# Column sums of w_out: eight slabs added on GpSimd ahead of two products, with a new table of keys

## The chip, the core and the metric

The program runs on one core of one Trainium2 chip. The metric is the device time of that core in microseconds (us), from the program's start to its end. The engines named here are TensorE (PE, with PEld for its weight loads), VectorE (DVE), ScalarE (ACT), GpSimd (POOL) and SyncE (SP), which issues nearly all DMA transfers here.

## What is computed

The kernel takes eight sequences of 3136 tokens by 256 features through a frequency-domain mix and then takes all 25088 tokens through a feed-forward layer.

```python
X = np.fft.rfft(x, axis=1)                 # 8 x 3136 x 256
Yr = Xr @ w_r - Xi @ w_i + b_r
Yi = Xr @ w_i + Xi @ w_r + b_i
Yr, Yi = soft_threshold(Yr, 0.01), soft_threshold(Yi, 0.01)
x = np.fft.irfft(Yr + 1j * Yi, n=3136, axis=1).reshape(25088, 256)
h = x @ w_in                               # 256 -> 1024
u = h * softmax(h)
ln = (u - mean(u)) / np.sqrt(var(u) + 1e-6) * g_ln
out = ln @ w_out                           # 1024 -> 256
```

`soft_threshold` shortens the name of three lines of the reference: sign times max(|y| - 0.01, 0).

## The kernel before

**Batches and tiles.** One batch is one sequence. The transforms are products with constant matrices in steps: `fwd1` (98 points, tiles of PSUM named `pf`, matrix `fa_s`), `fwd2` (32 points, matrix `fb`), the mix with `w_hi` and `w_lo`, the threshold, `inv1` (matrix `gb`, and `gs_s` for the last unit) and `inv2` (matrix `iaf_s` or `ia_s`), which fills a ring of token columns, `ring_hi` and `ring_lo`. Batch 0's transforms use the PSUM name `pb`, later ones `pf`. Each of 196 heads then takes 128 tokens out of the ring: `moe_head` makes `h` in two halves of 512 columns (six products each, PSUM name `ph`), VectorE finds the peak (`nm`), ScalarE the exponential (`u`, `se`), VectorE the product with it (`u`, `su`). `moe_turn` splits `u` into two float16 parts (`lh` on ScalarE, `ll` on GpSimd) that DMA transposes into `th` and `tl`. `moe_tail` multiplies these with `wout` in 24 products (PSUM name `po`) and scales the result (`o`). Data of 32 bits are carried as two 16-bit parts throughout, so most products come in threes.

**The first 130 us.** Batch 0 runs alone there, and the weights are made ready beside it. `fwd1_plain` of batch 1 is cut in eight chunks of `x` (tile `xt`, four buffers, shared with batch 0's bins) with two float32 products `pf<-xt,fa_s` each; `note_peak` reads each chunk for its peak, `x_scale` turns the peaks into a scale (`top`, a transpose on TensorE, then `v`, a product with `ones` that spreads it over the partitions). `moe_w_in` loads w_in in four pieces and `finish_w_in` splits it (`win_hi`, `win_lo`, `win_low`) when its peak is known (`wpeak`, `wtop`, `win_un`, `win_sc`). `moe_w_out` loads w_out in four pieces of two slabs, unpacks each with six VectorE instructions (on `lh`, `junk` and `ll`) and a GpSimd product, and multiplies the rows by `g_ln` (`gt`) on ScalarE. The four pieces lie in buffers named `th`, `tl`, `th`, `tl`.

**`finish_w_out`.** ScalarE takes the peak of each piece (`ll,mx`), `power_of_two` makes a scale of the four peaks through two small TensorE products with `wpeak` and `wtop`, and TensorE sums all 1024 rows of w_out into the column sums (eight float32 products `pf<-th,ones` and `pf<-tl,ones`). A float32 product leaves two MATMUL records in the trace. ScalarE writes the scaled sums into `o`; then each piece is scaled on ScalarE, GpSimd subtracts `o` from it, ScalarE casts the result to `wout[..., 0, :]` and GpSimd subtracts this for `wout[..., 1, :]`. No `po` product can start before the parts of `wout` that it reads are written.

**What sets the order.** Every operation carries a key (`nc.key`, from the table `KEYS`). A planner walks the operations by its own estimates of their lengths, takes for each engine the startable one with the smallest key within a patience of 50 ns, and writes each engine's program in the order found. Each engine then runs its own program strictly in that order and waits on semaphores where an input is not there. Buffers rotate by name: `u` has four, which w_in, the pieces of raw w_out and the heads share; `lh` and `ll` two each; `ph` may hold five of the eight PSUM banks, `po` two.

Of the kernel before, what the change touches and what calls it, by code (L numbers as in the profile page):

```python
# [12 lines left out]
F32 = mybir.dt.float32  # L13
# [28 lines left out]
def fft_constants():  # L42
# [73 lines left out]


KEYS = dict(
    slack_w=11.86, slack_1=3.28, slack_2=-1.08, gain=-179.81, xsc=-159.5, ssc=-155.78,
    b0=-187.72, b0_step=5.79, b0_mix=5.43, b0_inv=-16.84, b0_last=-31.78, in0=-155.58,  # L120
    in1=-179.39, in_end=-57.71, out=-132.55, out_step=3.47, out_peak=-55, out_sum=-54.6,
    out_end=-61.34, mixw=-54.7, a1=-96.85, a1_step=-0.23, a2=-73.62, a2_gap=-14.18, a=8.09,
    a_gap=10.32, b1=-74.41, b1_gap=4.59, b=-3.9, b_gap=1.01, f_mix=0, f_inv=0, back=-1.42,
    turn=1.77, tail=3.62,
)
K = KEYS.__getitem__

# [359 lines left out]
def fft_mix_solu_kernel(ctx: ExitStack, tc, x, w_r, w_i, b_r, b_i, w_in, w_out, g_ln, fa, iaf, fa16, fb, fs, gb, gs, ia, out):  # L487
    nc = Plan(tc.nc)
    B, _, D = x.shape
    FF = w_in.shape[1]  # L490
    P = 128
    ND = D // P
    NF = FF // P
# [10 lines left out]
    mp = Pool(ctx.enter_context(tc.tile_pool(name="mp", bufs=2)), 2)  # L504
# [3 lines left out]
    def front_psum(b):  # L508

        return banks.tile("pf" if b else "pb")  # L510
# [16 lines left out]
    ones = const.tile([P, P], F32, name="ones")  # L527
# [615 lines left out]
    pw = banks.tile("po")  # L1143
# [21 lines left out]
    pw = front_psum(0)  # L1165
# [3 lines left out]
    gain = const.tile([P, 1], F32, name="gain")  # L1169
# [33 lines left out]
    pw = front_psum(0)  # L1203
    nc.tensor.matmul(pw, ones[:1], bias_row.rearrange("p r e -> p (r e)"), start=True, stop=True)
    nc.scalar.copy(bias_t[:, :2].rearrange("p r e -> p (r e)"), pw)
    pw = front_psum(0)
# [43 lines left out]
    def power_of_two(peaks, un, sc, k):  # L1250

        top = sp.tile([P, 1], F32, name="wpeak", bufs=2)
        nc.vector.tensor_reduce(top, peaks, AX.X, ALU.max)
        pw = banks.tile("pf")
        nc.tensor.transpose(pw[:1, :P], top, ident)
        top = sp.tile([1, 1], F32, name="wtop", bufs=2)
        nc.vector.tensor_reduce(top, pw[:1, :P], AX.X, ALU.max)
        nc.vector.tensor_scalar(top, top, 2.0**-100, None, ALU.max)
        nc.vector.tensor_scalar(top.bitcast(U32), top.bitcast(U32), 0x7F800000, None, ALU.bitwise_and)
        pw = banks.tile("pf")  # L1260
        nc.tensor.matmul(pw[:, :1], ones[:1], top, start=True, stop=True)
        nc.vector.tensor_scalar(un, pw[:, :1], k, None, ALU.mult)
        nc.vector.tensor_scalar(sc.bitcast(U32), un.bitcast(U32), -1.0, float(254 << 23), ALU.mult, ALU.add)

    def moe_w_out():

        wo_s = [mp.tile([P, 2, D], F32, name=("th", "tl")[j % 2], bufs=3) for j in range(NF // 2)]
        rows = mp.tile([P, D], F32, name="o", bufs=2)[:NF, :P]
        nc.hold(raw[0, 3])
        nc.sync.dma_start(rows, g_ln.rearrange("(f p) -> f p", p=P))  # L1270
        pw = banks.tile("pf")
        nc.tensor.transpose(pw[:, :NF], rows, ident[:NF, :NF])
        gt = const.tile([P, NF], F32, name="gt")
        nc.vector.tensor_copy(gt, pw[:, :NF])
        for f in range(0, NF, 2):
            nc.key = K("out") + f * K("out_step")
            load_wide(wo_s[f // 2], w_out[f * P : (f + 2) * P].rearrange("(f p) e -> p f e", p=P), raw[0, 3])
            for i in (f, f + 1):
                row = wo_s[i // 2][:, i % 2]
                nc.scalar.activation(row, row, AF.Copy, scale=gt[:, i : i + 1])  # L1280
        return wo_s

    def finish_w_out(wo_s):

        nc.key = K("out_peak")
        mx = sp.tile([P, NF // 2], F32, name="mx", bufs=1)
        for j, half in enumerate(wo_s):
            junk = mp.tile([P, HF], BF16, name="ll", bufs=2)
            nc.scalar.activation(junk, half.rearrange("p f e -> p (f e)"), AF.Abs, accum_out=mx[:, j : j + 1])
        scale = sp.tile([P, 2], F32, name="scale", bufs=1)  # L1290
        power_of_two(mx, unscale, scale[:, :1], 2.0**-13)
        nc.vector.tensor_scalar(scale[:, 1:], scale[:, :1], 1.0 / FF, None, ALU.mult)
        nc.vector.tensor_scalar(unscale, unscale, 1e3 * W_SCALE, None, ALU.mult)
        nc.key = K("out_sum")
        pw = banks.tile("pf")
        with nc.together():
            for j in range(NF):
                nc.tensor.matmul(pw[:, :D], ones, wo_s[j // 2][:, j % 2], start=j == 0, stop=j == NF - 1)
        cm = mp.tile([P, D], F32, name="o", bufs=2)
        nc.scalar.activation(cm, pw[:, :D], AF.Copy, scale=scale[:, 1:])  # L1300

        nc.key = K("out_end")
        for j, half in enumerate(wo_s):
            fs = slice(2 * j, 2 * j + 2)
            nc.scalar.activation(half, half, AF.Copy, scale=scale[:, :1])
            for i in range(2):
                nc.gpsimd.tensor_sub(half[:, i], half[:, i], cm)
            nc.scalar.copy(wout[:, fs, 0], half)
            nc.gpsimd.tensor_sub(wout[:, fs, 1], half, wout[:, fs, 0])
# [42 lines left out]
    nc.key = K("out")  # L1352
    wo_s = moe_w_out()
    finish_w_out(wo_s)
    nc.key = K("mixw")
    later_mix_weights()
# [48 lines left out]
```

## Time and profile before

| | us |
|---|---|
| median of three runs (1524.37 to 1527.14) | 1526.11 |
| the profiled execution, whole | 1526.09 |
| its span, first to last instruction | 1524.3 |
| PE busy in the span | 1500.1 |
| DVE / ACT / POOL busy in the span | 1279.9 / 1245.1 / 1143.7 |

The profile is of one execution. A timeline row gives start, duration, engine, operation with what it writes and reads, and in brackets how long the engine sat idle before it and what ended that. A PE row's duration includes its drain, so the time that a product occupies the engine is read from the distance between starts. A row of the windows gives one stretch with each engine's busy time, the granted TensorE clock as a share of the higher of its two levels (2.4 and 1.2 GHz), and the DMA engines' mean busy share.

### The profile page before, as it was taken

To read this page: it belongs to the slowest core of one execution; us is meant where nothing else is said; L and a number is where in the kernel's file an instruction comes from. 1 tells how busy PE (TensorE), PEld (TensorE's weight loads), DVE (VectorE), ACT (ScalarE), POOL (GpSimd) and SP (SyncE) were. 2 spreads that over 40 slices of the span, in tenths; PEclk is the share of its full clock that TensorE was granted. 3 is DMA by queue.
4 is the path that set the end of the run, shared out by engine and by line. 5 is a ranking of instruction groups with operands and counts; after the bars stand their busy time and mean duration, and the time that the engine had idled before them with its cause. 6 is when DMAs were issued, how large, how long until landed. Compare 5 with 4: busy or idle time off the path is not lost.

```text
span 1524.3 us, 42130 instructions
## 1 busy us (share of the span) xinstructions
PE 1500.1 (98%) x15375; PEld 1060.9 (70%) x15375; DVE 1279.9 (84%) x3068; ACT 1245.1 (82%) x2548; POOL 1143.7 (75%) x1848
## 2 busy tenths in 40 slices
PE   6989999999999999999999999999999999999998
PEld 3446777667766777677766777667776777766676
DVE  5888899889998898978898888988989788776674
ACT  5789887998789878987888777887879788788886
POOL 0658998677977888569966788667986698867776
PEclk8989999999999999999999999999999999999999
DMA  8776977999679986999689996899769976687776
GB/s 265 226 225 154 172 168 175 240 233 222 162 169 229 233 192 141 260 216 215 143 171 234 233 189 142 185 246 225 158 140 213 224 143 114 140 174 140 143 129 115
DMA packets 531588, 285.69 MB, mean 187 GB/s; under 512 B 426500, under 2 KB 504688, under 8 KB 531380
## 3 DMA queue, kind: packets, MB, share of 16 engines
q1 hardware_dynamic: 530932, 281.39, 83.8%
q8 instruction: 120, 1.97, 0.6%
q10 hardware_dynamic: 448, 1.61, 0.4%
q14 instruction: 88, 0.72, 0.2%
HBM read 103.07 MB, written 77.07 MB: 118 GB/s over the span
## 4 chain that ended last, share of the span: by engine, by line
PE 90%; DVE 3%; ACT 2%; POOL 2%; DMA 2%; issue 1%; SPq 0%; DVEq 0%; ACTq 0%; POOLq 0%
PE po L375 31%; PE ph L375 31%; PE pf L375 24%; PE pb L375 3%; DMA u<-in_x_dram 1%; DVE xl L375 1%; POOL ll L375 1%; DVE nm L375 0%; DMA u<-in_moe_w_out_dram 0%; DVE u L375 0%; POOL wout L375 0%; DVE av L375 0%; DMA xt<-in_x_dram 0%; ACT w_hi L375 0%; POOL a L375 0%
## 5 line engine op out<-in xcount | busy, mean ns | idle before, releaser
L375 POOL TENSOR_TENSOR ll<-u,lh 128x1024 f16<-128x1024 f32 x196 | 424.9, 2168 | 88.8 <-ACT lh L375 86.8
L375 PE MATMUL po<-wout,th 128*128 128x256 f16 x3136 | 374.5, 273 | 0.0
L375 ACT ACTIVATE u<-ph,m,hsb 128x512 f32<-128x512 f32 x384 | 297.2, 782 | 77.2 <-DVE m L375 77.0
L375 DVE TENSOR_REDUCE nm<-ph 128x1 f32<-128x512 f32 x392 | 266.8, 687 | 104.9 <-PE ph L375 103.8
L375 PEld LDWEIGHTS <-th 128*128 128x128 f16 x3136 | 303.6, 98 | 56.6 <-issue 0.8
L375 DVE SCALAR_TENSOR_TENSOR u<-ph,ch,u 128x512 f32<-128x512 f32 x392 | 284.6, 748 | 38.5 <-ACT u L375 29.0
L375 PE MATMUL ph<-win_hi,ring_hi 128*128 128x512 f16 x768 | 291.2, 379 | 0.7 <-DVE u L375 0.5
L375 PE MATMUL ph<-win_low,ring_lo 128*128 128x512 f16 x768 | 291.0, 379 | 0.0
L375 PE MATMUL ph<-win_lo,ring_hi 128*128 128x512 f16 x768 | 291.0, 379 | 0.0
L375 ACT CAST lh<-u 128x1024 f16<-128x1024 f32 x196 | 206.6, 1055 | 50.9 <-DVE u L375 49.7
L375 PEld LDWEIGHTS <-ring_hi 128*128 128x128 f16 x1536 | 148.5, 98 | 137.4 <-issue 1.8
L375 ACT ACTIVATE junk<-u,total 128x1024 bf16<-128x1024 f32 x196 | 227.6, 1161 | 10.9 <-POOL total L375 10.3
L375 PE MATMUL po<-wout,tl 128*128 128x256 f16 x1568 | 203.3, 273 | 0.8 <-DMA tl<-ll 0.8
L375 POOL TENSOR_TENSOR y<-yt,yc 128x512 f32<-128x512 f32 (+1 forms) x104 | 134.5, 1297 | 52.7 <-ACT yt L375 26.4
L375 PEld LDWEIGHTS <-tl 128*128 128x128 f16 x1568 | 151.9, 98 | 24.0 <-DMA tl<-ll 1.1
L375 PE MATMUL pf<-w_hi,Xh 128*128 128x256 f16 x532 | 145.0, 273 | 0.0
L375 PE MATMUL pf<-w_lo,Xh 128*128 128x256 f16 x532 | 145.0, 273 | 0.0
L375 PE MATMUL pf<-w_hi,Xl 128*128 128x256 f16 x532 | 145.0, 273 | 0.0
L375 PEld LDWEIGHTS <-ring_lo 128*128 128x128 f16 x768 | 75.1, 98 | 90.7
L375 PEld LDWEIGHTS <-Xh 128*128 128x128 f16 x1168 | 113.4, 98 | 34.7 <-issue 3.3
L375 POOL TENSOR_SCALAR se<-se,se 128x1 f32<-128x1 f32 x196 | 62.7, 320 | 95.6 <-ACT u L375 43.5
L375 ACT ACTIVATE o<-po,r 128x256 f32<-128x256 f32 x196 | 95.3, 486 | 43.1 <-PE po L375 37.9
(207 smaller groups left out, 2766.9 us busy)
## 6 DMA issues: line engine op xcount, KB each, us to landing
xt<-in_x_dram SPq DMA_DIRECT2D x104, 392.0 KB
zt<-s SPq DMA_DIRECT2D x56, 392.0 KB
s<-zout SPq DMA_DIRECT2D x42, 512.0 KB
s<-av SPq DMA_DIRECT2D x48, 392.0 KB
bin<-s SPq DMA_DIRECT2D x36, 512.0 KB
out_dram<-o SPq DMA_DIRECT2D x128, 96.0 KB
out_dram<-o SPq DMA_DIRECT2D x136, 64.0 KB
out_dram<-o SPq DMA_DIRECT2D x128, 32.0 KB
```

The lines of the kernel that those rows point to most:

```text
L375: getattr(engine, name)(*args, **kw)
```

## The change

The eight slabs lie in four tiles of 128 x 512. GpSimd adds the tiles in pairs and the two results into one (three additions of 128 x 512 float32), into two buffers named `lh`. TensorE then multiplies `ones` with the two slabs that are left: two float32 products, that is four MATMUL records, where there were eight and sixteen. The scale of the sums and everything behind it are unchanged. Beside it 27 of the 35 keys have new values, which the planner turns into a new order.

```diff
 KEYS = dict(
...
-    b0_step=5.79, b0_mix=5.43, b0_inv=-16.84, b0_last=-31.78, in0=-155.58,
...
-    turn=1.77, tail=3.62,
+    slack_w=19.86, slack_1=24.51, slack_2=0.37, gain=-96.89, xsc=-70.56, ssc=-37.95, b0=-91.08,
...
         nc.key = K("out_sum")
+        cs = [mp.tile([P, 2, D], F32, name="lh", bufs=2) for _ in range(2)]
+        for i in range(2):
+            nc.gpsimd.tensor_add(cs[i], wo_s[i], wo_s[i + 2])
+        nc.gpsimd.tensor_add(cs[0], cs[0], cs[1])
         pw = banks.tile("pf")
         with nc.together():
-            for j in range(NF):
-                nc.tensor.matmul(pw[:, :D], ones, wo_s[j // 2][:, j % 2], start=j == 0, stop=j == NF - 1)
+            for j in range(2):
+                nc.tensor.matmul(pw[:, :D], ones, cs[0][:, j], start=j == 0, stop=j == 1)
         cm = mp.tile([P, D], F32, name="o", bufs=2)
         nc.scalar.activation(cm, pw[:, :D], AF.Copy, scale=scale[:, 1:])
```

Three places show how the order moves.

TensorE at the end of the front, from the last `fwd1_plain` products of batch 1 to the first head (`th,ones` and `tl,ones` are the sums, `wpeak` and `wtop` the two products of w_out's peak, `iaf_s,zt` batch 0's `inv2`, `ph` a head). Before:

```order
L375 MATMUL pf<-xt,fa_s 98x512 x3
L375 MATMUL pf<-th,ones 128x256 x2
L375 MATMUL pf<-tl,ones 128x256 x2
L375 MATMUL pf<-th,ones 128x256 x2
L375 MATMUL pf<-tl,ones 128x256 x2
L375 MATMUL pf<-ident,wpeak 1x128
L375 MATMUL pf<-iaf_s,zt 128x98 x8
L375 MATMUL pf<-wtop,ones 128x1
L375 MATMUL pf<-iaf_s,zt 128x98 x8
L375 LDWEIGHTS ring_hi
L375 MATMUL ph<-win_hi,ring_hi 128x512
```

The same place now (`v` is batch 1's scale):

```order
L374 MATMUL pb<-yh,gs_s 128x256
L374 MATMUL pf<-xt,fa_s 98x512 x3
L374 MATMUL pf<-v,ones 128x2
L374 MATMUL pf<-xt,fa_s 98x512 x2
L374 MATMUL pf<-iaf_s,zt 128x98 x16
L374 LDWEIGHTS ring_hi
L374 MATMUL ph<-win_hi,ring_hi 128x512
```

The heads start ahead of everything that belongs to w_out: `wpeak` stands behind 18 `ph` products, the sums (`pf<-lh,ones 128x256 x2`) behind 24, `wtop` behind 30, and the first `po` behind 66 where it stood behind 60. Both programs have 24 `iaf_s,zt` products ahead of that `po`.

GpSimd, from the last product that unpacks w_out to the first parts of `wout`. Before:

```order
L375 TENSOR_TENSOR tl<-tl,ll 128x512
L375 TENSOR_TENSOR th<-th,o 128x256 x2
L375 TENSOR_TENSOR tl<-tl,o 128x256 x2
L375 TENSOR_TENSOR wout<-th,wout 128x2x256
L375 TENSOR_TENSOR wout<-tl,wout 128x2x256
```

The same place now (`lh` holds the added slabs; `se`, `a`, `total` and `ll<-u,lh` belong to the first head):

```order
L374 TENSOR_TENSOR th<-th,ll 128x512
L374 TENSOR_TENSOR lh<-th 128x512
L374 TENSOR_TENSOR lh<-tl 128x512
L374 TENSOR_TENSOR lh<-lh 128x512
L374 TENSOR_SCALAR se_1766<-se_1766,se_1778 128x1
L374 TENSOR_SCALAR a<-se_1766,ch,hsb 128x1
L374 TENSOR_TENSOR total<-su_1782,su_1790 128x1
L374 TENSOR_TENSOR a<-a 128x1
L374 TENSOR_TENSOR ll<-u,lh 128x1024
L374 TENSOR_TENSOR th<-th,o 128x256 x2
```

Three additions and the first head's split now stand between the last unpacked piece and the subtraction of `o`.

ScalarE around the four peaks of w_out (`ll,mx`). Before:

```order
L375 ACTIVATE ll,mx<-tl 128x512
L375 ACTIVATE tl<-tl,gt 128x256 x2
L375 ACTIVATE ll,mx<-th 128x512
L375 ACTIVATE ll,mx<-tl 128x512
L375 ACTIVATE ring_hi<-pf 128x384
L375 ACTIVATE last_hi<-pf 128x4x2
L375 ACTIVATE ring_hi<-pf 128x384
L375 ACTIVATE last_hi<-pf 128x4x2
L375 ACTIVATE ring_hi<-pf 128x384
L375 ACTIVATE th<-th,scale 128x512
```

The same place now:

```order
L374 ACTIVATE th<-th,gt 128x256 x2
L374 ACTIVATE last_hi<-pf 128x4x2
L374 ACTIVATE ll,mx<-th 128x512
L374 ACTIVATE ll,mx<-tl 128x512
L374 ACTIVATE ll,mx<-th 128x512
L374 ACTIVATE ll,mx<-tl 128x512
L374 ACTIVATE u,se_1766<-ph,m,hsb 128x512
L374 ACTIVATE u,se_1778<-ph,m,hsb 128x512
L374 CAST lh<-u 128x1024
L374 ACTIVATE bin<-bin,sc 128x4x256
L374 ACTIVATE th<-th,scale 128x512
```

All four peaks stand behind the last piece's `gt` step, where two of them stood ahead of it, and the first head's exponentials and cast stand between the peaks and the scaling.

## Rows read from the trace of the kernel before

**Rows 1.** The page: busy time by engine, and the chain's shares by engine.

```profile
PE 1500.1 (98%) x15375; PEld 1060.9 (70%) x15375; DVE 1279.9 (84%) x3068; ACT 1245.1 (82%) x2548; POOL 1143.7 (75%) x1848
PE 90%; DVE 3%; ACT 2%; POOL 2%; DMA 2%; issue 1%; SPq 0%; DVEq 0%; ACTq 0%; POOLq 0%
```

**Rows 2.** Windows: stretch, length, then busy time of each engine, clock, DMA.

```profile
97.00:107.00 10.00, 8.05 (x14) 2.87 (x13) 9.66 (x38) 9.05 (x17) 4.93 (x5) 0.52 0.53 176
116.00:131.00 15.00, 15.00 (x81) 8.12 (x80) 13.90 (x40) 15.00 (x33) 12.13 (x20) 1.00 0.66 179
200.00:300.00 100.00, 100.00 (x1096) 72.91 (x1095) 90.65 (x219) 80.79 (x165) 76.03 (x121) 1.00 0.85 193
```

**Rows 3.** Timeline of PE, 92 to 131 us: start, duration, instruction, [idle before].

```profile
92.40 1.10 PE L375 MATMUL pf<-xt,fa_s 98*98 98x512 f32 x2
...
96.75 0.32 PE L375 MATMUL pf<-ident,top 98*1 98x98 f32 x1 [1.91 <-DVE win_un L375]
96.87 1.91 PE L375 MATMUL pf<-xt,fa_s 98*98 98x512 f32 x2
100.73 0.55 PE L375 MATMUL pf<-v,ones 1*128 1x2 f32 x2 [1.95 <-DVE v L375]
...
107.63 1.03 PE L375 MATMUL pf<-th,ones 128*128 128x256 f32 x4
108.49 1.03 PE L375 MATMUL pf<-tl,ones 128*128 128x256 f32 x4
...
111.70 2.03 PE L375 MATMUL pf<-iaf_s,zt 98*128 98x98 f32 x16
113.66 0.38 PE L375 MATMUL pf<-wtop,ones 1*128 1x1 f32 x2
...
115.83 0.38 PE L375 MATMUL ph<-win_hi,ring_hi 128*128 128x512 f16 x1
...
130.52 1.91 PE L375 MATMUL po<-wout,th 128*128 128x256 f16 x16
```

**Rows 4.** The chain in order of time: start, us, what; one head's products.

```profile
164.31 2.59 PE ph L375 x12
```

**Rows 5.** Timeline of SP's queue, 80 to 110 us.

```profile
87.35 0.32 SPq L375 DMA_DIRECT2D xt<-in_x_dram  x1
...
96.30 0.37 SPq L375 DMA_DIRECT2D u<-in_moe_w_out_dram  x1
...
106.53 1.29 SPq L375 DMA_DIRECT2D zt<-s2f  x2
```

**Rows 6.** Timeline of DVE, 92 to 110 us.

```profile
92.84 1.22 DVE L375 TENSOR_REDUCE peaks<-xt 98x1 f32<-98x1024 f32 x1 [0.17 <-DMA xt<-in_x_dram]
93.98 0.42 DVE L375 TENSOR_SCALAR lh<-lh 128x512 uint32<-128x512 uint32 x1
...
99.62 0.89 DVE L375 TENSOR_SCALAR lh<-lh 128x512 uint32<-128x512 uint32 x1
100.43 0.15 DVE L375 TENSOR_SCALAR v<-v 1x2 uint32<-1x2 uint32 x1
...
105.25 0.69 DVE L375 SCALAR_TENSOR_TENSOR ll<-u,lh 128x512 uint32<-128x512 uint32 x1
...
106.50 3.37 DVE L375 SCALAR_TENSOR_TENSOR win_lo<-u,win_sc,win_hi 128x1024 f16<-128x1024 f32 x2
```

**Rows 7.** Timeline of ACT, 99 to 119 us.

```profile
99.37 1.15 ACT L375 ACTIVATE win_hi<-u,win_sc 128x1024 f16<-128x1024 f32 x1
...
110.43 0.62 ACT L375 ACTIVATE ll<-tl 128x512 bf16<-128x512 f32 x1
...
115.53 0.71 ACT L375 ACTIVATE th<-th,scale 128x512 f32<-128x512 f32 x1
...
117.98 0.45 ACT L375 ACTIVATE o<-pf,scale 128x256 f32<-128x256 f32 x1
```

**Rows 8.** Timeline of POOL, 92 to 133 us.

```profile
92.41 1.39 POOL L375 TENSOR_TENSOR th<-th,ll 128x512 f32<-128x512 f32 x1 [0.63 <-DVE ll L375]
...
106.02 1.56 POOL L375 TENSOR_TENSOR tl<-tl,ll 128x512 f32<-128x512 f32 x1 [2.84 <-DVE ll L375]
118.51 1.41 POOL L375 TENSOR_TENSOR th<-th,o 128x256 f32<-128x256 f32 x2 [10.93 <-ACT o L375]
...
127.35 1.15 POOL L375 TENSOR_TENSOR wout<-tl,wout 128x512 f16<-128x512 f32 x1
...
130.56 2.13 POOL L375 TENSOR_TENSOR ll<-u,lh 128x1024 f16<-128x1024 f32 x1
```

More of the change, by code (lines that the diff above doesn't have):

```diff
@@ L118 @@
 KEYS = dict(
[L119 to L123, printed above, removed]
-    turn=1.77, tail=3.62,
+    slack_w=19.86, slack_1=24.51, slack_2=0.37, gain=-96.89, xsc=-70.56, ssc=-37.95, b0=-91.08,
+    b0_step=4.51, b0_mix=-36.3, b0_inv=-32.77, b0_last=95.45, in0=-88.04, in1=-91.89,
+    in_end=-3.66, out=-49.24, out_step=-2.48, out_peak=0.97, out_sum=-48.17, out_end=-11.01,
+    mixw=-183.57, a1=-38.5, a1_step=1.91, a2=-3, a2_gap=-9.29, a=8.09, a_gap=10.32, b1=-1.49,
+    b1_gap=8.96, b=-3.9, b_gap=1.01, f_mix=0, f_inv=0, back=-7.99, turn=1.77, tail=3.62,
 )
```

## Prediction

> **What bounds the kernel now.** First the page: TensorE is busy for 1500.1 of 1524.3 us and holds 90% of the chain that ended last [rows 1]. Then the windows: from 200 to 300 us it is busy for all of 100.00 us at the full granted clock [rows 2], and the later windows read alike. So from the first heads on the time is the sum of TensorE's products, which the change leaves as they are, and only the first 131 us can gain or lose. I read those engine by engine in the timelines. TensorE waits in the last part of the front: 1.91 us ahead of `top` at 96.75, 1.95 us ahead of `v` at 100.73 [rows 3]; and from 97 to 107 us its granted clock is 0.52, the lower of its two levels [rows 2], so that a pair of `xt` records takes 1.91 us and not 1.10 [rows 3]. After that it has work without a break: sums from 107.63, `inv2` from 111.70, heads from 115.83, the first `po` at 130.52 [rows 3]. That first `po` is where I compare the two programs: what stands behind it is the same work on a busy TensorE. The profiled execution took 1526.09 us, the median of the runs is 1526.11, so I count from 1526.1.
>
> **The products that go.** Four records of a sum take 108.49 - 107.63 = 0.86 us [rows 3], so 16 take 3.46 and four 0.87: TensorE has 2.6 us less to do. They lay on its path, back to back with what stands around them. This is the whole of what the change can give by itself. Whether it arrives depends on when the first `po` can start.
>
> **What is computed at that point.** Ahead of the first `po` stand 60 head products before and 66 now, and 24 of `inv2` in both. Twelve head products take 2.59 us [rows 4], so the new program has 6 x 0.216 = 1.3 us more behind it there. With T for the new start of the first `po` the gain is 130.52 + 1.3 - T.
>
> **T, step by step**, along w_out's chain, since TensorE alone would be ready earlier (last step). *Top.* To the end of batch 0's last mix both orders have nearly the same products, one `xt` product more and one group of `inv1` less; I take the same time, 89.4 us. TensorE now meets `top` ahead of the last `inv1` group. `top` needs the peak of chunk 7, whose load waits for a buffer that the same product frees as before: issued 87.35 [rows 5], read at 92.84 for 1.22 us [rows 6]. So `top` comes at 94.0, not 96.75, and TensorE waits there about 2.5 us in place of shorter waits that add up to as much. *Fourth piece of w_out.* Its load stands behind the store of batch 0's last unit: `inv1` 0.7, four evictions 1.1, `win_hi` 1.05 (1.15 less overlap, [rows 7]), the eviction 0.3, two issues 0.8: 97.9, not 96.30 [rows 5]. *VectorE* has some ten instructions of the second and third pieces (0.42 to 0.69 us each, [rows 6]) ahead of `v`, which comes at 100.8 (before 100.43, [rows 6]); then one `win_lo` 1.69 (half of 3.37, [rows 6]), small ones 1.0, five of the fourth piece 2.1, the other `win_lo` 1.69 and `ll` 0.6: 108.0, where `ll` ended at 105.94 [rows 6]. *GpSimd* unpacks it in 1.3 us: 109.3 (before 107.58, [rows 8]). *ScalarE* needs 0.9 for `gt` and now all four peaks behind it, 4 x 0.67: 112.9, where the last one ended at about 111.1 [rows 7]. *TensorE*: `wpeak`, then 12 head products (2.6) and the new sums (0.87) stand ahead of `wtop`: 117.0, where it was 113.66 [rows 3]. *Scale*: before, ScalarE came to it 1.9 us after `wtop`, at 115.53, and `o` was its fifth result, ending at 118.43 [rows 7]; now it waits for the scale with nothing between (0.7) and `o` is its second: 118.7. *The additions* cost nothing on this chain if each takes the 1.28 us that GpSimd needs for a product of this shape (1.39 at 92.41, [rows 8], less overlap): 3.9 us from about 110 to 114, in the 10.93 us that GpSimd sat idle for `o` [rows 8]. They delay the sums only if they end behind 24 head products, about 114.7. GpSimd's first head split (2.13 us at 130.56 before, [rows 8]) also moves into that hole and ends near 119.4. *wout*: from the first subtraction to the last part took 128.5 - 118.51 = 10.0 us [rows 8], now 119.4 + 10.0 = 129.4; the last part is read 1.3 us after the first `po`. *TensorE itself*: heads from about 108.3 (its `inv2` input follows the store at 97.8 by some six us, as loads do here, and takes 3.9 us at the rate of [rows 3], 111.70 to 113.66 for eight), then 66 head products 14.3, `inv2` 2.0, sums and small ones 1.1: 125.7. But five banks of `ph` are freed by ScalarE's exponentials, ScalarE is busy for 15.00 of 15.00 us there already before [rows 2], and it now casts `wout` between them: I put the last bank at 128 and T at 129.3.
>
> Gain: 130.52 + 1.3 - 129.3 = 2.5 us, so 1526.1 - 2.5 = **1523.6 us**. It is nearly the 2.6 us of the products: the earlier heads do not add to it, because w_out is ready no earlier than before.
>
> **Bounds of what no row shows.** T cannot be under 125.7, TensorE's own sum (gain 6.1). Upward, additions at twice their length and the low clock on `inv2` are priced below. My walk joins a dozen rows with waits that I estimate; I give it 1.6 us either way.
>
> **Where a rule speaks against the change.** At 99.62 an `lh<-lh` of VectorE took 0.89 us beside a running GpSimd instruction, at 93.98 only 0.42 [rows 6]. The Trainium skill, "GPSIMD Engine Reference", section "Key points", says why: GpSimd shares its SBUF interfaces with VectorE and contends with instructions in a two-port mode or with two SBUF inputs. By that rule the additions are not free, though VectorE's work there (ring, peaks, reads of PSUM) has few such instructions.
>
> **The rivals.** *A, the hole closes further* (chance 0.24, 1520.6). The low clock lies wholly where TensorE waits anyway, chunk 7 lands as fast as it can, and ScalarE frees the banks sooner: T = 126.3, gain 5.5. For it: 3.3 us of the front go to the low clock alone (four to five pairs at 0.8 us more, [rows 3]), and the new order puts five fewer products behind `v`. Against it: `v` comes no earlier. *B, given back* (0.20, 1525.8). The additions stretch from 1.28 to about 2 us, as contention did to the 0.42 us instruction, and end at 116.5; the sums stand ahead of `wtop` on TensorE, so the scale slips by about 2 us, T = 131.5, gain 0.3. Against it: the few two-input instructions just named. *C, slower* (0.16, 1530). The low stretch of the clock, 10 us long at 97 to 107 [rows 2], begins after the wait for `v` instead, and covers `inv2` and the first heads: 3.9 us become 7.8, and the 12 head products ahead of `wtop` take 2.6 us more. The fourth piece's `gt` stands behind the last ring eviction on ScalarE, so all of it lands on the scale: T = 135.8, a loss of 4.0. It turns into a loss when T passes 131.8, and one that can be measured from 134.9. For it: TensorE's waits now lie at 91.2 to 94.0, near 98.4 to 100.8 and ahead of `inv2`, later than before. The Trainium skill, "TensorE: Matmul & The Clock Gate", section "What's actually happening", says that the transition point varies; no run here shows how much. That the sums are not shortened is no rival: the order has two products in place of eight.
>
> **How the numbers follow.** About 0.2%, 3.05 us, is what a measurement of this kernel can tell from no change, so faster means under 1523.0 and slower over 1529.2. The forecast has 0.40, with 1522.0 to 1525.2 as its own range; a third of it lies under 1523.0. Faster: 0.24 + 0.14 = 0.38. Slower: most of C, 0.13. Same: the rest, 0.49. The range reaches from the middle of A to the lower part of C, 1519.6 to 1528.6, and leaves out 0.07 below and 0.13 above.
>
> **What would show each step.** Four sum records of 0.86 us together, behind 24 head products. `top` near 94, `v` near 100.8 and the heads from about 108, against 115.83. The last peak of w_out near 113, `wtop` near 117, `o` near 118.7, the last part of `wout` near 129.4 and the first `po` near 129. If the additions take over 1.6 us each, or TensorE waits at the sums, B is at work; if the granted clock is low under `iaf_s,zt` or the first `ph`, C. A `po` before 127 means A. The prediction is wrong in kind if the first `po` comes on time and the gain is lost later, by waits of heads in the windows from 131 us on, which I take as none.

## The result, and the profile after

The median of six runs is 1535.26 us (1530.52 to 1536.73), that of the kernel before in the same sessions 1527.47 (1524.37 to 1528.42): a ratio of 1.0053 [1.0043, 1.0063], some 8 us slower. The forecast was 1523.6 with a range to 1528.6; the measured time lies above the range and on the side that was given 0.13. The profiled execution took 1534.58 us.

The page of the kernel after, busy time by engine, as in [rows 1]:

```profile
PE 1503.3 (98%) x15363; PEld 1062.2 (69%) x15363; DVE 1285.6 (84%) x3068; ACT 1242.8 (81%) x2548; POOL 1157.5 (76%) x1851
```

TensorE has twelve records fewer (x15363 for x15375) and is busy 3.2 us longer. The windows of after say why (columns as in [rows 2], the clock is the third number from the end):

```profile
97.00:107.00 10.00, 6.43 (x65) 3.06 (x66) 9.78 (x26) 9.47 (x22) 6.22 (x6) 1.00 0.83 255
107.00:121.00 14.00, 12.36 (x44) 8.42 (x43) 9.20 (x36) 7.79 (x21) 3.94 (x4) 0.51 0.72 239
...
200.00:300.00 100.00, 99.46 (x1179) 72.37 (x1178) 92.96 (x210) 82.32 (x170) 76.97 (x117) 1.00 0.75 158
```

From 97 to 107 us the granted clock is now 1.00, where it was 0.52. The low stretch has moved to 107 to 121 us (0.51, the lower of the two levels), and there it covers `inv2` and the first heads. From 200 us on the two programs read alike. TensorE's timeline of after, the rows that answer [rows 3]:

```profile
93.40 0.28 PE L374 MATMUL pb<-w_hi,Xh 128*128 128x256 f16 x1
...
97.98 0.24 PE L374 MATMUL pf<-ident,top 98*1 98x98 f32 x1 [1.18 <-DVE wtop L374]
...
105.97 0.35 PE L374 MATMUL pf<-v,ones 1*128 1x2 f32 x2 [1.72 <-DVE v L374]
106.25 3.00 PE L374 MATMUL pf<-xt,fa_s 98*98 98x512 f32 x4
110.90 7.12 PE L374 MATMUL pf<-iaf_s,zt 98*128 98x98 f32 x32 [1.64 <-DMA zt<-s2f]
117.81 0.63 PE L374 MATMUL ph<-win_hi,ring_hi 128*128 128x512 f16 x1
...
124.52 1.03 PE L374 MATMUL pf<-lh,ones 128*128 128x256 f32 x4
...
126.77 0.38 PE L374 MATMUL pf<-wtop,ones 1*128 1x1 f32 x2
...
136.62 1.15 PE L374 MATMUL po<-wout,th 128*128 128x256 f16 x9
138.05 0.60 PE L374 MATMUL po<-wout,th 128*128 128x256 f16 x4 [0.28 <-POOL wout L374]
139.33 0.49 PE L374 MATMUL po<-wout,th 128*128 128x256 f16 x3 [0.68 <-POOL wout L374]
```

`inv2`'s 32 records take 110.90 to 117.81, 6.9 us, where [rows 3] give half as many in 1.96; a head product then lasts 0.63 and not 0.38, until 120.36. The first `po` comes at 136.62. Less the 1.3 us for six more head products, it is 136.62 - 131.8 = 4.8 us late. Waits for `wout` add 0.28 + 0.68, a wait of a later `po` for `u` at 161.28 adds 1.58, and the window from 200 to 300 us lacks 0.54: 7.9 of the 8.5 us between the spans. Where the last two waits come from was not followed.

Where the 4.8 come from is read in one window per kernel, from the start of `inv2` to the first `po`: before, after, and a version of the new program at the full clock (`xh_warm`, below).

```profile
111.70:130.52 18.82, 18.82 (x110) 11.81 (x111) 15.96 (x49) 16.56 (x38) 11.65 (x19) 1.00 0.63 186
```

```profile
110.90:136.62 25.72, 25.72 (x121) 16.64 (x122) 18.69 (x59) 17.96 (x44) 15.62 (x19) 0.81 0.78 240
```

```profile
111.03:132.51 21.48, 21.10 (x123) 12.83 (x122) 17.99 (x58) 17.92 (x44) 15.57 (x19) 1.00 0.94 260
```

In before and after TensorE is busy for all of it, so the first `po` comes when `inv2` can start plus the sum of the products behind it. `inv2` starts 0.8 us earlier. The sum is 25.72 for 18.82, 6.9 more: 1.3 are the six heads, some 4.6 the clock (TensorE is busy for 21.10 at the full one), 0.86 the four sum records, which now stand on this side of `inv2`, and 0.1 `wpeak`. Before, the sums stood on the other side, where TensorE would have waited (`cut_sums`, below).

The other engines of after: VectorE, SyncE's queue, ScalarE, GpSimd, each in its own fence, for [rows 5 to 8].

```profile
99.52 0.13 DVE L374 TENSOR_SCALAR v<-v 1x1 f32<-1x1 f32 x1
...
102.39 1.82 DVE L374 TENSOR_SCALAR lh<-lh 128x512 uint32<-128x512 uint32 x2
...
105.68 0.15 DVE L374 TENSOR_SCALAR v<-v 1x2 uint32<-1x2 uint32 x1
```

```profile
102.63 0.47 SPq L374 DMA_DIRECT2D s2f<-zs  x1
103.19 0.54 SPq L374 DMA_DIRECT2D u<-in_moe_w_out_dram  x1
...
104.92 1.08 SPq L374 DMA_DIRECT2D zt<-s2f  x2
```

```profile
118.44 0.90 ACT L374 ACTIVATE th<-th,gt 128x256 f32<-128x256 f32 x2
...
121.22 0.61 ACT L374 ACTIVATE ll<-tl 128x512 bf16<-128x512 f32 x1
...
128.38 0.45 ACT L374 ACTIVATE o<-pf,scale 128x256 f32<-128x256 f32 x1
```

```profile
111.98 1.27 POOL L374 TENSOR_TENSOR th<-th,ll 128x512 f32<-128x512 f32 x1 [3.84 <-DVE ll L374]
119.47 1.26 POOL L374 TENSOR_TENSOR lh<-th 128x512 f32<-128x512 f32 x1 [6.23 <-ACT last_hi L374]
...
138.12 1.16 POOL L374 TENSOR_TENSOR wout<-tl,wout 128x512 f16<-128x512 f32 x1
```

Between two tiny steps of `v`, at 99.52 and 105.68, VectorE unpacks w_out for 6 us. The fourth load of w_out and the load of `zt` both stand behind the store of batch 0's last unit (`zs`) at 102.63. The last piece's `gt` step comes 5.2 us after its unpacking ends (111.98 + 1.27 to 118.44), right behind the fourth ring eviction. The three additions take 1.26 to 1.27 us each.

A further loss lies early, at 46 us. TensorE, then ScalarE, of after, then ScalarE of before:

```profile
48.72 0.39 PE L374 MATMUL pb<-w_hi,Xh 128*128 128x512 f16 x1 [2.06 <-ACT Xh L374]
```

```profile
45.84 0.60 ACT L374 ACTIVATE Xh<-pb 128x512 f16<-128x512 f32 x1 [1.13 <-PE pb L374]
46.34 0.71 ACT L374 ACTIVATE yc<-yt,sc 128x512 f32<-128x512 f32 x1
...
48.08 0.58 ACT L374 ACTIVATE Xh<-pb 128x512 f16<-128x512 f32 x1
```

```profile
45.47 1.09 ACT L375 ACTIVATE Xh<-pb 128x512 f16<-128x512 f32 x2 [1.13 <-PE pb L375]
```

In the new order three steps of the threshold (`yc`, `yh`, `yt`) stand ahead of the second `Xh`, and the `Xh` are the evictions that the next mix waits for. The key of the mixes (`b0_mix` from 5.43 to -36.3) is the likely reason, since it now puts a mix some eight steps ahead of the `fwd2` beside it where it stood one step behind; no run changes it alone. TensorE waits 2.06 us, and afterwards some eight products run at the lower level. At 84.44 another wait for `Xh` costs 2.50.

### The profile page after: what moved, and what is told of

Its sections match the earlier page's. It is cut to its first block, busy times and chain, and to the rows that moved or that the text cites. A ratio compares the mean times of both kernels' runs of the same rounds, so it can differ in the third digit from the quotient of the medians.

```text
span 1532.8 us, 42144 instructions
## 1 busy us (share of the span) xinstructions
PE 1503.3 (98%) x15363; PEld 1062.2 (69%) x15363; DVE 1285.6 (84%) x3068; ACT 1242.8 (81%) x2548; POOL 1157.5 (76%) x1851
## 4 chain that ended last, share of the span: by engine, by line
PE 86%; DVE 4%; ACT 3%; POOL 3%; issue 1%; DMA 1%; SPq 0%; ACTq 0%; DVEq 0%; POOLq 0%
PE po L374 30%; PE ph L374 30%; PE pf L374 23%; PE pb L374 3%; POOL y L374 1%; POOL ll L374 1%; ACT u L374 1%; ACT junk L374 1%; POOL yl L374 1%; DVE u L374 1%; DVE nm L374 1%; DVE Xl L374 1%; DVE yt L374 0%; DVE yc L374 0%; DVE bin L374 0%
```

## The experiments

Every kernel was timed in five rounds beside the kernel before; ratios are to that.

**The two halves.** `sum_alone` has the new sum with the old table, `keys_alone` the new table with the old sum of eight products.

```diff
-        cs = [mp.tile([P, 2, D], F32, name="lh", bufs=2) for _ in range(2)]
-        for i in range(2):
-            nc.gpsimd.tensor_add(cs[i], wo_s[i], wo_s[i + 2])
-        nc.gpsimd.tensor_add(cs[0], cs[0], cs[1])
...
-            for j in range(2):
-                nc.tensor.matmul(pw[:, :D], ones, cs[0][:, j], start=j == 0, stop=j == 1)
+            for j in range(NF):
+                nc.tensor.matmul(pw[:, :D], ones, wo_s[j // 2][:, j % 2], start=j == 0, stop=j == NF - 1)
```

That is `keys_alone` against the kernel after; `sum_alone` is the reverse against the kernel before.

> The table of numbers of before, with the three additions and the four-record sum of after. Theory K (the new order of the front costs the time, the new sum pays): the last mix of batch 0 starts at about 88 us as in before, 12 sum records of 0.216 us go, and the time falls by up to 2.6 us, to 1524.5 to 1526.5. Rival S (the sum itself costs: the additions wait for all eight slabs, and the chain to the output scale gets longer by their 3.9 us): 1529 or more, with TensorE waiting at the sums.

> The table of numbers of after, with the sixteen sum records of before and no additions. Theory K: the front is as late as in after (last mix of batch 0 near 93.4 us, inv2 at the low clock), and the time is that of after or up to 2.6 us more: 1535 to 1539. Rival S: without the additions the loss goes, 1525 to 1529.

Measured: `sum_alone` 1.0098 [1.0085, 1.0111], 1541.3 us; `keys_alone` 1.0081 [1.0068, 1.0093], 1539.8. Each half loses more than both together. With the new table the new sum saves about 4 us (1.0081 to 1.0053); with the old table the same sum costs 15. In `keys_alone` the sixteen records stand behind `inv2` and six heads, with TensorE busy around them:

```profile
118.72 1.03 PE L374 MATMUL pf<-th,ones 128*128 128x256 f32 x4
```

They end at 122.17, and the first `po` comes at 139.74. There the twelve records do lie on the path and cost the 2.6 us; a wait of 2.06 ahead of a head at 135.84 adds to that, and a shorter low stretch under `inv2` (5.7 us for 6.9) takes some of it off. TensorE in `sum_alone`, at the place where the sixteen records stood before:

```profile
112.12 5.44 PE L375 MATMUL pf<-iaf_s,zt 98*128 98x98 f32 x24 [4.74 <-DMA zt<-s2f]
```

The sums had lain between the last `xt` product and `inv2`. Without them TensorE stands still for 4.74 us, `inv2` starts no earlier than before (112.12, [rows 3] have 111.70), and then runs at half rate: 24 records in 5.2 us. The first `po` comes at 139.03, behind 66 heads too, 7.2 us late. Some 6 us of waits follow after 130 us (1.5 in the kernel before), among them 2.8 for `av` on VectorE between 300 and 800 us. So the 15 us are not the empty place alone: with the new sum the planner moves other work as well, and what the sum is worth depends on the order around it. The later waits were not followed.

**The removed products by themselves.** `cut_sums` keeps the order of the kernel before and leaves out twelve of the sixteen records, so its column means are those of two slabs of eight; `cut_warm` puts fourteen products of ones into the hole.

```diff
-                for name, args, kw in op.calls:
+                for name, args, kw in op.calls[: 2 if op.seq == 443 else None]:
```

> Before, in before's own order, with 12 of the 16 sum records left out (the two products of the first slab stay, so the column means are those of two slabs of eight) and nothing put in their place. Theory H (the sums lay in a hole: TensorE had nothing else to do while inv2's input was under way): inv2 starts at 111.5 to 112.5 as in before, TensorE waits some 3 us ahead of it, the granted clock is low under it (6 to 7 us for 32 records, not 4) and under the first heads, and the time is not lower, 1526 to 1531. Rival P (the step of the prediction: the 16 records lie on the path): inv2 starts 2.6 us earlier, the time falls by 2.6 us, to 1523.7.

> The run without 12 of the 16 sum records (the column means are those of two slabs of eight), with 14 products of ones, whose results nobody reads, in the 3 us that TensorE waited in their place, ahead of the peak's transpose. Theory C (what the missing records cost there is the clock alone: in the wait TensorE falls to the lower level, and inv2 and the first heads run at it): the granted clock stays full from 107 to 120 us, inv2's two halves take 2.0 us each again, the first po is at 130 to 132, and the time is that of before, 1526 to 1527.5. Rival (the missing records also cost by the order behind them): 1529 or more.

Measured: `cut_sums` 1.0036 [1.0022, 1.0049], 5.5 us by the medians, `cut_warm` 1.0000 [0.9991, 1.0009]. TensorE's timeline and the window of 107 to 118.5 us, first in `cut_sums`, then in `cut_warm`:

```profile
110.88 0.27 PE L375 MATMUL pf<-ident,wpeak 128*1 128x128 f32 x1 [2.95 <-DVE wpeak L375]
111.48 2.79 PE L375 MATMUL pf<-iaf_s,zt 98*128 98x98 f32 x16 [0.33 <-DMA zt<-s2f]
...
114.71 3.74 PE L375 MATMUL pf<-iaf_s,zt 98*128 98x98 f32 x16
...
135.18 1.91 PE L375 MATMUL po<-wout,th 128*128 128x256 f16 x16
```

```profile
107.00:118.50 11.50, 8.22 (x41) 7.26 (x40) 6.07 (x18) 6.53 (x19) 0.07 (x1) 0.74 0.78 240
```

```profile
108.09 3.29 PE L374 MATMUL pf<-ones 128*128 128x128 f32 x28
...
111.48 2.03 PE L378 MATMUL pf<-iaf_s,zt 98*128 98x98 f32 x16
...
113.75 2.03 PE L378 MATMUL pf<-iaf_s,zt 98*128 98x98 f32 x16
...
130.30 1.91 PE L378 MATMUL po<-wout,th 128*128 128x256 f16 x16
```

```profile
107.00:118.50 11.50, 11.50 (x82) 9.22 (x81) 7.30 (x21) 8.47 (x24) 0.35 (x2) 1.00 0.75 230
```

This is the cleanest pair of the study. In both `inv2` starts at 111.48, within 0.3 us of the kernel before, so 2.6 us of products taken away ahead of it give nothing. In `cut_sums` two things hold it there: `wpeak`, which stands ahead of `inv2` in TensorE's order and waits 2.95 us for the last peak of w_out, and behind it 0.33 us for `zt`. With the hole, the clock falls and `inv2` takes 2.79 + 3.74 us for 2.03 + 2.03, and the first `po` comes at 135.18. With work of no use in the hole it comes at 130.30, as before. The removed products were a filler in this order: worth 0 on the path, and some 5 us as cover for the clock.

**Two losses of the new table.** `xh_first` moves the two late `Xh` evictions on ScalarE back up in the planner's order, `warm` puts 20 products of ones into the new program, 8 ahead of `v`'s product and 12 ahead of `inv2`; `xh_warm` does both.

```diff
+        for seq, at in [(151, 149), (268, 266)]:
+            op = next(o for o in order if o.seq == seq)
+            order.remove(op)
+            order.insert(next(i for i, o in enumerate(order) if o.seq == at) + 1, op)
...
+                for _ in range({547: 8, 920: 12}.get(op.seq, 0)):
+                    bank = View(op.calls[0][1][0].tile, (0, 128), np.arange(512), F32)
+                    engine.matmul(bank[:, 384:].placed(), self.ones.placed(), self.ones.placed(), start=True, stop=True)
```

> After, with two evictions Xh of batch 0 moved up on ScalarE, each to right behind the Xh before it: the one that ended at 48.65 us and the one that ended near 84.4. Nothing else moves. Theory K, the part in the front: TensorE's waits of 2.06 and 2.50 us for Xh shrink to under 1 and under 0.5, the low stretch at 49.4 to 52.0 us (1.6 us lost) goes or shrinks, the last mix starts at 88.5 to 90 in place of 93.4, and the time falls by 3.5 to 5 us, to 1530.5 to 1532. Rival Z (the front's gain is taken back: inv2's input and w_out's pieces come by transfers that are no earlier): inv2 starts at 110 or later and the time stays within 1 us of 1535.

> After, with 20 more products of the matrix of ones with itself, whose results nobody reads: 8 ahead of the product of v, 12 ahead of the first product of inv2, each 0.21 us at full clock, in stretches in which TensorE waits (1.72 and 1.64 us, with 0.95 us of low clock on the xt records between). Theory C (the low clock on inv2 and the first six heads costs 3.0 + 1.3 us on the path): the granted clock is full from 106 to 120 us, 32 records of inv2 take 3.9 us and not 6.9, the first head starts near 115, and the time falls by 3 to 4.5 us, to 1531 to 1532.5. Rival W (the end of the front is set by w_out's chain on VectorE, GpSimd and ScalarE, the clock costs nothing): the heads start earlier, wout is no earlier, 1534.5 to 1536.

> After with both earlier edits: the two evictions Xh moved up, and the 20 products of ones. Theory Z+C (the front's 4.2 us arrive only as 1.2, since inv2's input and v wait for other things; the clock is a cost by itself): inv2 at 109.6, full clock, 32 records in 4 us, first head near 113.7, first po near 131.5 to 132, 1528 to 1530. Rival (the two gains are the same gain, both by keeping TensorE busier): no lower than the run with the products of ones alone, 1531.

Measured: `xh_first` 1.0045 [1.0033, 1.0057], `warm` 1.0038 [1.0024, 1.0051], `xh_warm` 1.0024 [1.0015, 1.0033]. In `xh_first` the last mixes come at 89.21 for 93.40, but `inv2` waits 2.86 us for `zt` and starts at 109.65, only 1.25 earlier; eleven head products behind it run at half rate where six did and a seventh in part, and the first `po` comes 1.0 earlier. So the front's gain is mostly taken back. TensorE in `warm`, then in `xh_warm`:

```profile
111.25 4.07 PE L377 MATMUL pf<-iaf_s,zt 98*128 98x98 f32 x32 [0.30 <-DMA zt<-s2f]
...
133.09 1.15 PE L377 MATMUL po<-wout,th 128*128 128x256 f16 x9
```

```profile
148.62 1.92 PE L381 MATMUL po<-wout,th 128*128 128x256 f16 x16 [0.68 <-DMA th<-lh]
157.22 1.91 PE L381 MATMUL po<-wout,th 128*128 128x256 f16 x16 [0.73 <-DVE u L381]
```

At the full clock `inv2` starts 0.35 later than in the kernel after and its 32 records still end 2.7 us earlier; the first `po` gains 3.5. `xh_warm` wins back 4.4 of 8 us by the ratios. Its span is 4.1 us above that of before: the first `po` is 0.7 late (132.51 against 131.8), the sums being on its path; it waits 1.0 for `wout`, and two later ones wait 1.4, for `u` and for a transpose. Those are 3.1 of the 4.1; the rest is not placed. Its `inv2` was expected at 109.6 and started at 111.03, without a wait, right behind the twelve products of ones. The load of `zt` went out at 103.67; by the 6.0 to 6.4 us from issue to `inv2` in the kernel after and `xh_first` it would have landed near 109.8 (an estimate). So here the filler itself stood in the way, by about 1.2 us (an estimate too).

**Moving w_out's chain up.** In the new program `o` comes ten microseconds later than before. `scale_first` moves the peak, the scale and the sums ahead of the heads (24 moves of the kind above), `all_three` joins it with `xh_warm`, `wout_too` also moves the rest of w_out's last pass up.

> After, with the chain to w_out's scale moved up: on ScalarE the last slab's gt, the four peaks and then scale and o ahead of the third and fourth ring evictions and the first exponentials; the additions follow gt on GpSimd; on TensorE the transpose of the peak behind 6 head products, the product of wtop and the new sums behind 12 (18, 30 and 24 in after). Theory O (with 30 head products queued ahead of it on TensorE the scale waits for the heads, and all of wout behind it): wtop at 122 to 123 in place of 126.8, o near 124.5 in place of 128.8, the first po near 132.5 to 133, the time lower by 3 to 4 us, 1530.5 to 1532. Rival Q (the heads that were moved behind cost as much, since ScalarE and VectorE are full): 1534 or more.

> After with all three edits together: Xh moved up, 20 products of ones, scale chain moved up. If the three costs are separate (front 1.2, clock 3.1, order of the scale 3.5): the first po at 128.5 to 130.5 and 1524.5 to 1527, level with before. If they overlap: 1528 or more.

> The run with all three edits, with the rest of w_out's last pass moved up as well: on ScalarE the other three scalings right behind o and the first two casts of wout behind the first two exponentials, on GpSimd the second slab's subtraction and the first two remainders ahead of the first head's split. Theory O2 (o was early for nothing since ScalarE's other scalings and casts stood behind exponentials; the last part of wout sets the first po): the last part of wout at 134 to 135.5 in place of 138.1, the first po near 131.5 to 132.5, 1528.5 to 1530. Rival Q: the heads that wait for GpSimd and ScalarE instead cost as much, 1532 or more.

Measured: 1.0050 [1.0038, 1.0063], 1.0039 [1.0026, 1.0051], 1.0068 [1.0056, 1.0081]. In all three it is the second case of the expectation that came. In `scale_first` the scale is there 6.4 us earlier (`wtop` at 120.41), and the last part of `wout` ends at 139.0, 0.3 earlier than in the kernel after: ScalarE's next scaling and the casts stood behind the heads' exponentials. The first `po` comes at 135.80, again right behind a TensorE that is busy from `inv2` on but for 0.53 us: w_out's chain did not set it. `all_three` has its first `po` at 134.90, 2.4 later than `xh_warm`: TensorE now waits 1.14 for `wpeak` (0.38 there), 0.56 for `last_lo` and 0.53 for a head's `ch`. When the casts are moved as well, the heads pay. TensorE in `wout_too`:

```profile
132.25 0.39 PE L381 MATMUL ph<-win_hi,ring_hi 128*128 128x512 f16 x1 [2.33 <-DVE ch L381]
```

TensorE waits for a head's VectorE steps, and ScalarE 4.12 us for the ring (131.77). Each of these orders served one of the two, the heads or w_out, and let the other wait; what could be won was no more than the waits of about 1 us for `wout`.

**The same means on the kernel before.** `before_warm` adds 16 products of ones to the kernel before, 8 ahead of `top` and 8 ahead of `v`, to lift its low clock of 97 to 107 us. `zt_early` keeps the old order, takes the new sum, puts batch 0's last unit ahead of w_out's slabs so that `zt` loads earlier, and fills TensorE's waits with 27 products of ones.

> Before, with 16 products of ones whose results nobody reads: 8 ahead of top's transpose, 8 ahead of the product of v, in TensorE's two waits of 1.9 us. Theory H (what TensorE does ahead of inv2's input is free in before): the granted clock is full from 97 to 107 us, the xt records end some 3 us earlier, inv2 still starts at 111.3 to 112 and the time stays within 1 us of before. Rival (the low clock there costs before its 3.3 us): 1523 to 1524.5.

> Before's own order with the new sum put into it by hand, and the hole ahead of inv2 closed from the other side: the last unit of batch 0 goes ahead of w_out's slabs on VectorE, ScalarE, GpSimd and TensorE, so that its store and inv2's loads go out some 5 us earlier; inv2 ahead of the peak's transpose, the four new sum records behind wtop and six head products; 27 products of ones in the waits. Theory H (the products pay once inv2's input no longer sets the heads): inv2 at 105.5 to 107.5, the first head near 111.5, wtop no later than 113.7, the first po at 128.5 to 130 with the same 60 head products ahead of it, 1523.5 to 1526. Rival (w_out's last part and ScalarE set the first po in before as well): 1526 or more.

Measured: `before_warm` 1.0019 [1.0010, 1.0027], `zt_early` 1.0005 [0.9993, 1.0016]. In `before_warm` the clock is 1.00 from 90 to 100 us, falls to 0.84 on average from 100 to 111 after a wait of 2.02 for `v`, and `inv2` waits 0.63 for its input, at 113.11. The time was to stay within 1 us and rose by 0.19%, more than the noise. The profiled execution does not say what the low clock cost the kernel before: its front is 1.4 us late already at the last mixes (89.48 for 88.05), ahead of the first product added, and `v` comes at 102.80 for 100.73. What it does show is that sixteen such products did not hold the clock there and gained nothing. `zt_early` is the best version with the new sum: 0.5% better than the change as made, level with the kernel before. Its load of `zt` was to go out some 5 us earlier and went out at 105.16, 1.4 earlier than before (106.53, [rows 5]). `inv2` starts at 109.32, but the first `po` comes at 130.53: five products of ones (ten records, 1.3 us) and the sums stand on TensorE behind `inv2`, and the last part of `wout` ends at 129.70. TensorE, GpSimd, then VectorE, in `zt_early`:

```profile
112.97 1.30 PE L378 MATMUL pf<-ones 128*128 128x128 f32 x10
```

```profile
109.84 2.24 POOL L389 TENSOR_TENSOR lh<-th 128x512 f32<-128x512 f32 x1
113.04 1.27 POOL L389 TENSOR_TENSOR lh<-tl 128x512 f32<-128x512 f32 x1 [0.96 <-ACT tl L386]
...
128.54 1.16 POOL L386 TENSOR_TENSOR wout<-tl,wout 128x512 f16<-128x512 f32 x1
```

```profile
108.79 4.38 DVE L386 SCALAR_TENSOR_TENSOR win_lo<-u,win_sc,win_hi 128x1024 f16<-128x1024 f32 x2
```

The first addition takes 2.24 us beside two `win_lo`, VectorE instructions that read two SBUF tiles and take 4.38 where two apart take 1.26 and 1.28 (`xh_warm`). The additions that stand alone take 1.27. No version came out ahead of the kernel before.

## Why the prediction was wrong

**The term of the sum: T.** The first `po` was put at 129.3 and came at 136.62, 7.3 us late. The walk set it by w_out's chain and let TensorE be "ready earlier", at 125.7. TensorE's own sum came to 136.6 and was the later of the two: 6.5 us from the late start of `inv2` (110.90, where heads from 108.3 ask for 104.4), some 4.6 from the low clock under it and the first heads. Behind the first `po` 3.1 us were lost (0.28 + 0.68 waiting for `wout`, 1.58 + 0.54 later) where the forecast had none. Between a gain of 2.5 us as forecast and a loss of 8.5 in the spans lie 11.0, and these two make up all but 0.6 of them.

**The products that go: the step that failed first.** "They lay on its path, back to back with what stands around them" and "the whole of what the change can give" took records without an idle gap for a path. They stood ahead of a product whose input came late: `zt`, issued at 106.53 [rows 5], while the sixteen records run from 107.63 to 111.09 and `inv2` starts at 111.70 [rows 3]; and ahead of `wpeak`, which waits for w_out's last peak. A busy engine hid two waits that were about as long. `cut_sums` and `cut_warm` show it: 0 and not 2.6 us, and 5 us lost when the place stays empty. "Back to back" in the timeline shows no wait because the wait was filled. In the new order the step would have held: there the sixteen records stand behind `inv2`, on the path (`keys_alone`).

**The same front.** "I take the same time, 89.4 us" for the end of the last mixes was wrong by 5.3 us: they start at 93.40 and end by 94.7. TensorE in the kernel before:

```profile
88.05 0.28 PE L375 MATMUL pb<-w_hi,Xh 128*128 128x256 f16 x1
```

The count of products was right; the ScalarE order of 40 to 90 us, which the new keys change too, was not read. The start of the front also differs between executions: 93.40 in the kernel after and 91.25 in `scale_first`, with the same order there, so a single trace tells it to about 2 us. Most of it did not reach the end: `xh_first` moves the mixes to 89.21 and is worth about 1 us.

**`v` and the loads.** `top` at 94.0 came at 97.98, 4 us late from the front. `v` was put at 100.8 with "some ten instructions" of unpacking ahead of it and came at 105.68: 4.0 of the 4.9 us are `top`'s, and the rest is that some of the ten took longer than put (1.82 for two at 102.39). The fourth w_out load, 97.9, came at 103.19; the 1.3 us beyond the front are on ScalarE, where an `av` copy (98.69) and the `yh` cast, which waits 0.53 for GpSimd's `y`, stand ahead of the four evictions. The input of `inv2` was put some six us behind the store of batch 0's last unit. SyncE's queue in the kernel before:

```profile
104.10 0.47 SPq L375 DMA_DIRECT2D s2f<-zs  x1
```

`inv2` started 7.6 us behind that store before and 8.3 behind it in the kernel after (102.63 to 110.90): the six us are the load alone, and it goes out 2.3 to 2.4 us behind the store. So the heads could not come at 108.3: `inv2` alone began at 110.90.

**The low clock, rival C.** Half of its mechanism is what happened: the low stretch begins after the wait for `v` and covers `inv2` and the first heads, with `gt` behind the last ring eviction. It had a chance of 0.16, T = 135.8 and 1530; the first `po` came at 136.62. That the two are so close is luck in part: C let the delay land on w_out's scale, and it was TensorE's own sum, with a late `inv2` that C did not have. Its sizes: `inv2` took 6.9 us for the 7.8 given, the heads 1.25 more for 2.6. `warm` prices the clock at 3.5 us of the first `po`, 3.1 of the spans and 2.3 by the ratios. The Trainium skill, "TensorE: Matmul & The Clock Gate", section "What's actually happening", is borne out in that activity releases the throttle: in `cut_warm` fourteen products whose result nobody reads kept 1.00 where the hole gave 0.74. I had seen where the waits would move and still gave this case the smallest chance.

**w_out's chain.** The peaks were to end at 112.9 and ended at 121.9: 4 us from what is late ahead of it, 5 from the wait of `gt` behind the slow ring evictions. `wtop` at 117.0 took the 18 heads ahead of `wpeak` as done when the peaks are; the heads began at 117.81 and not at 108.3, and behind 30 of them and the sums `wtop` came at 126.77. `o` at 118.7 became 128.8. Yet T was not set there: w_out cost 1.0, the two waits behind the first `po`, and moving its chain alone (`scale_first`) changed the time by no more than the noise.

**Right.** The four sum records take 0.86 us, behind 24 heads. The additions took 1.26 to 1.27 us each, not stretched: rival B did not happen in this order. Its mechanism exists: in `zt_early` an addition took 2.24 us beside `win_lo`, about the 2 us that I had put, and the trace there agrees with the rule cited (the Trainium skill, "GPSIMD Engine Reference", section "Key points": GpSimd contends with VectorE instructions of two SBUF inputs). The stretch did not last to the sums there and cost nothing that shows.

**Open.** Why two later `po` in `xh_warm` wait 1.4 us, the one us of its gap that is not placed, the 1.58 + 0.54 us that the kernel after loses after 140 us, and the waits that `sum_alone` meets after 130 us are not explained. What the low clock of 97 to 107 us costs the kernel before is not shown either. That an order exists in which the new sum gains is not excluded; `zt_early` came closest, with 1.3 us of its own filler on the path.

## What to carry over

Before work is taken off a busy engine, ask when the input of the next product arrives: rows without a gap may be a filler ahead of an input that is late, and then the removal gives nothing and can cost the clock of what follows. Where a change comes with a new table of keys, walk every engine's order from the start and not only at the place that the edit is about. Price such an edit with both tables, since here the same new sum saved 4 us with one and cost 15 with the other.

## What was not expected of the hardware

In `cut_sums` a wait of 2.95 us ahead of one small product and `inv2` went with a granted clock of 0.74 over 11.5 us, where it was 1.00 with the wait filled, and the first `po` came 4.9 us later: nearly twice the work removed. Products whose result nobody reads cost nothing in time there (1.0000 [0.9991, 1.0009]) and held the clock at its upper level. That is no rule: in `before_warm` sixteen of them did not hold it and the time rose by 0.19%, and in `xh_warm` the filler outlasted the wait.
